# Operand start, one-word transfers ahead of weight reads, and regrouped sums in a linear-attention and two-FFN kernel

## The chip, the cores and the metric

The kernel runs on one core of a Trainium2 chip. The metric is the device time of one execution in microseconds. The engines are TensorE (PE in the rows; PEld is its weight load), VectorE (DVE), ScalarE (ACT), GpSimd (POOL) and SyncE (SP), which issues most transfers; POOL issues some on a queue of its own.

## The reference

All is fp32. Attention gives 4608 rows of 512 columns, and two feed-forward layers with squared ReLU follow, 512 to 2048 to 512 columns each:

```python
q_s = softmax(q, axis=-1); k_s = softmax(k, axis=seq)      # 8 x 8 heads, 576 x 64
kv  = einsum('bhsd,bhse->bhde', k_s, v)
x   = einsum('bhsd,bhde->bhse', q_s, kv)                    # -> 4608 x 512
x   = (max(x @ w_in1, 0) ** 2) @ w_out1
y   = (max(x @ w_in2, 0) ** 2) @ w_out2
```

## The kernel before

**Tiling.** The 4608 rows are worked in 9 blocks of 512 (numbered 0 to 8). The four weight matrices are called 0 to 3 in the order of use. Each is cut into 8 parts, and `W2_5` is part 5 of matrix 2, the second layer's first. A tile of the trace carries such a name: `W` a weight operand, `G` a hidden operand (`G0_8_7` is layer 0, block 8, part 7), `x` the second layer's input operand (`x0_0` and `x0_1` are the two halves of block 0), `v` the first layer's.

**Stages.** An opening stage does the attention and the first layer's first product in plain form for blocks 0 to 5; blocks 6 to 8 go through a *first crossing* (PSUM tiles `n`). Then come the *first sweep* (tiles `y`, matrix 1, about 474 to 816 us), the *second crossing* (tiles `m`, matrix 2, 816 to 1165 us, into which the last sums of the first sweep reach), and the *second sweep* (`y`, matrix 3, to the end). The blocks of the crossing and of the sweep after it follow each other without a gap, so that at 816 us the sums of block 8 of the first sweep and the first products of block 0 of the second crossing are worked together.

**Products.** Each 2 x 2 block product is formed from seven products in place of eight (`LEFT`, `RIGHT`, and the order of the products). Three PSUM banks hold a unit of a crossing: product 1; products 2, 4 and 7; products 5, 3 and 6 (`BANK`). A bank is used by the next product once its sum has been copied out. The name `m2_0_2` says: bank of product 2, block 0, unit 2; a unit is two weight parts, so unit 2 uses `W2_4` and `W2_5`. Each fp32 operand is split into a high and a low part and each product has three matmuls for each piece, so that a product of a crossing is 12 matmuls of 256 columns (`first_mm`, `passes`); all of these matmuls are issued in line 448.

**Operands.** An operand has seven combinations, 14 x 256 words with high and low. `combine` makes one out of a loaded tile: three additions of DVE into a scratch tile (`comb_add`, lines 97 to 106: 512, 512 and 256 columns), two copies of ACT that round to the high part (`comb_hi`, line 119: 512 and 1280 columns), two subtractions of DVE for the low part (`comb_lo`, line 125: 512 and 1280). `comb_hi` also chooses at which word of its buffer an x, v or G operand starts (`PLAIN` is 8, `EARLY` 4, `LATE` 40). The v operands start at `PLAIN`, and their row 0 of the high part, that of RIGHT index 0, starts four words earlier by a view `low`.

**Weights.** Some weight operands (`KEPT`, among them W2_0, W2_1, W2_2, W2_3, W2_5 and W2_7) were made earlier and stored ready in DRAM. `get_operand` (line 190) reads one, 1.8 MB, by a DMA of POOL's queue (`W<-o` in the rows) into one of eight slots. Two of these reads, and two for matrix 3, must not pass the load of a G tile in time; `touch` (line 186) stands ahead of each, an addition of one element by POOL that waits for the G tile. The other parts (W2_4, W2_6) are loaded as raw tiles by SP (`qx<-w`, line 177) and combined.

**Sums.** A unit's products become sums by ACT's copies of a bank (`copy`, line 476), POOL's or DVE's addition of two copies (`both`, line 479), DVE's `rest` (line 482), `summed` (line 488) and `plus` (line 518), POOL's `plus2` (line 521), then ReLU and square on ACT and a store.

**Order.** The kernel doesn't leave the order to a scheduler of the compiler: `schedule` is a list planner that is written in the kernel. Every operation is an `Op` with an engine, a cost in ns, a due time (`T` holds the stages' starts), the operations that it follows (`after`), the buffers that it uses (`Place`), for transfers their size (`lands`), `port` (whether it is counted as sharing DVE's and POOL's port) and `held` (a time before which it isn't taken). Each engine in the plan takes the ready operation of least due time, and the code is written out in that order for all engines, each of which then works strictly in order.

Of the kernel before, what the change touches and what calls it, by code (L numbers as in the profile page):

```python
# [48 lines left out]
def linear_attention_two_relu2_ffn(ctx: ExitStack, tc: tile.TileContext, q0, k0, eye, qh, kh, vh, wio, out):  # L49
# [58 lines left out]
    def comb_hi(key, q, x, tag):  # L108
        if key not in hls:
            if key[0] in "Gxv":  # L110
                t = pool.tile([P, 14 * HB + SHIFT], F32R, name=key, tag=tag)
                o = LATE + 4 * (key in ("G1_0_0", "G1_0_1", "G1_2_0")) if key[:2] == "G1" else EARLY if key == "G0_0_0" or key[:2] == "x0" else PLAIN
                hls[key] = t[:, o:o + 14 * HB].rearrange("p (a b n) -> p a b n", a=2, b=7)
                if key[0] == "v":
                    low[key] = t[:, o - 4:o - 4 + 2 * (HB + 4)].rearrange("p (a n) -> p a n", a=2)[:, :, :HB]
            else:
                hls[key] = pool.tile([P, 2, 7, HB], F32R, name=key, tag=tag)
        r, src = (slice(0, 2), q[:, 0:4:3]) if x == 0 else (slice(2, 7), cfs[key])
        nc.scalar.activation(out=low[key] if x == 0 and key in low else hls[key][:, 0, r], in_=src, func=AF.Copy)  # L119
# [63 lines left out]
    def put_operand(f, a):  # L183
        nc.sync.dma_start(out=ready_w[f, a], in_=f32(hls.pop(f"S{f}_{a}")))

    def touch(f, a, key):
        one = pool.tile([P, 1], F32, name=f"touch{f}_{a}", tag="kvm")
        nc.gpsimd.tensor_tensor(out=one, in0=gq[key][:, 0, 0:1], in1=gq[key][:, 0, 0:1], op=ALU.add)  # L188

    def get_operand(f, a, tag):  # L190
        hls[f"W{f}_{a}"] = pool.tile([P, 2, 7, HB], F32R, name=f"W{f}_{a}", tag=tag)
# [265 lines left out]
    def first_mm(l, j, u, i, place):  # L457

        k, o = (l, j, u), BANK[i]
        if i == o:  # L460
            m[k, o] = bank(place, f"{'nm'[l]}{i}_{j}_{u}")
        for s in range(2):
            w = hls[f"W{2 * l}_{2 * u + s}"]
            terms = []
            for kk in range(2):
                x, c = hls[f"{'vx'[l]}{j}_{kk}"], slice(kk * P, (kk + 1) * P)
                high = x[:, 0, RIGHT[i]] if l or RIGHT[i] else low[f"v{j}_{kk}"][:, 0]
                terms.append((w[:, 0, LEFT[i], c], w[:, 1, LEFT[i], c], high, x[:, 1, RIGHT[i]]))
            passes(m[k, o][:, s], terms, start=i == o and s == 0)

# [116 lines left out]
    def act(n, ps=False):  # L587
        return n * 0.823 + (174 if ps else 209)

    def dve(n):  # L590
        return n * 1.07 + 140
# [127 lines left out]

    combined = {}  # L720

    def combine(key, tag, due, engines, q, place, after, cfplace, new):

        hl = Place(tag)
        n = (512, 512, 256)
        adds = [op(e, gps(n[x]) if e == "POOL" else dve(n[x]), due - 5200 + 10 * x, lambda x=x, e=e: comb_add(key, q(), x, e, new), after, [place, cfplace], port=True)
                for x, e in enumerate(engines)]
        h0 = op("ACT", act(512), due - 4500, lambda: comb_hi(key, q(), 0, tag), after, [hl, place])
        h1 = op("ACT", act(1280), due - 3000, lambda: comb_hi(key, q(), 1, tag), adds, [hl, cfplace])
        l0 = op("DVE", dve(512), due - 2500, lambda: comb_lo(key, q(), 0), [h0], [hl, place], port=True)  # L730
        l1 = op("DVE", dve(1280), due - 1500, lambda: comb_lo(key, q(), 1), [h1], [hl, cfplace], port=True)
        combined[key] = [l0, l1], hl
# [73 lines left out]
    def weights(f, a, due):  # L806

        if (f, a) in KEPT:
            place = Place(slot_of(a))
            b = behind.get((f, a))  # L810
            if b:
                assert b in g_loads, (f, a)
            seen = op("POOL", 200, due - 9000, lambda: touch(f, a, b), [g_loads[b]], [g_place[b]]) if b else None
            l = op("POOL", 1400, due - 9000, lambda: get_operand(f, a, slot_of(a)), [*kept[f, a], seen, begun.get((f, a))], [place], lands=1792, port=False)
            combined[f"W{f}_{a}"] = [l], place
            return
        beside = Place(slot_of(a + 1)) if f == 0 and a not in (2, 7) else None
        place, new = quad_place("quad", 0, beside) if beside else quad_place(("qx", "qa")[a % 2] if f else "qc")
        after = [dma(due - 12000, lambda: get_w(f, a, new), 512, stashed[f, a], [place])]
        if beside:  # L820
            cf = Place("five", parent=beside), lambda: beside.area(4 * HB, 5 * HB).rearrange("p (a n) -> p a n", n=HB)
        else:
            cf = cf_place(("cf", ("att1", "att2")[a % 2], "att1", "att1")[f])
        combine(f"W{f}_{a}", slot_of(a), due, ("DVE",) * 3, lambda: wfs[f, a], place, after, *cf)

    kept, begun = {}, {}

# [172 lines left out]
    def first(l, j, u):  # L1000
        k, d = (l, j, u), when(2, j, u) if l else when(0, j, 4 * u)
        M, bk, tt = {}, {}, {}
        chain = chains[l]
        wx = [combined[f"W{2 * l}_{2 * u + s}"] for s in range(2)] + [combined[f"{'vx'[l]}{j}_{kk}"] for kk in range(2)]
        ready = [o for os, _ in wx for o in os]
        hl = [h for _, h in wx]
        bk = {i: Place("ps") for i in (2, 5, 1)}
        g = 1360

        def mm(i, due, after=()):  # L1010
            b = bk[BANK[i]]
            M[i] = op("PE", g, due, lambda: first_mm(l, j, u, i, b), [*ready, *after], [*hl, b])
            return M[i]

        def copy_of(i, due):
            tt[f"s{i}"] = t_place[k, f"s{i}"] = Place("t")
            return op("ACT", act(512, 1), due, lambda: copy(k, i), [M[i]], [tt[f"s{i}"], bk[i]])

        def out_of(q, o, due):
            if q in (0, 3):  # L1020
                o = op("ACT", act(512), due, lambda: relu(k, q), [o], [tt[q]])
            if l:
                o = op("ACT", act(512), due + 700, lambda: square(k, q), [o], [tt[q]])
            stored.setdefault((l, j, 2 * u), []).append(dma(due + 1500, lambda: put_g(k, q), 256, [o], [tt[q]]))
            stored[l, j, 2 * u + 1] = stored[l, j, 2 * u]


        mm(2, d, [chain[-3]] if chain else [])
        c2 = copy_of(2, d + g)
        mm(5, d + g, [M[2]])  # L1030
        c5 = copy_of(5, d + 2 * g)
        if (l, j) == (0, FIRST):
            s = op("DVE", dve(512), d + 3 * g, lambda: both(k, "DVE"), [c2, c5], [tt["s5"], tt["s2"]], port=True)
        else:
            s = op("POOL", gps(512), d + 3 * g, lambda: both(k), [c2, c5], [tt["s5"], tt["s2"]])
        mm(1, d + 4 * g, [M[5], *chain[-1:]])
        if (l, j, u) == (1, 0, 1):
            begun[2, 7] = M[1]
        e = op("DVE", dve(512), d + 5 * g, lambda: rest(k), [s, M[1]], [tt["s5"], bk[1]])
        for x, (i, q, c, y, f) in enumerate(((4, 2, c2, 7, 0), (3, 1, c5, 6, 3))):  # L1040
            o = BANK[i]
            mm(i, d + (5 + x) * g, [c, M[1 if x == 0 else 4]])
            tt[q] = t_place[k, q] = Place("t")
            r = op("ACT", act(512, 1), d + (6 + x) * g, lambda q=q, o=o: plain(k, q, o), [M[i]], [tt[q], bk[o]])
            out_of(q, r, d + (6 + x) * g + 3000)
            dy = d + (UNIT if l else SHORT / 4) + (2 + x) * g
            mm(y, dy, [r])
            tt[f] = t_place[k, f] = Place("t")
            r = op("DVE", dve(512), dy + g, lambda f=f, o=o: summed(k, f, o), [M[y], e], [tt[f], bk[o], tt["s5"]])
            out_of(f, r, dy + g + 3000)  # L1050
        chain[:] = [M[3], M[7], M[6]]
# [4 lines left out]
    def second(l, j, a):  # L1056
# [35 lines left out]
        for q, i, o, po in ((0, 7, 2, p21), (3, 6, 1, p12)):  # L1092
            tt[q] = t_place[k, q] = Place("t")
            if quick:
                y = op("DVE", dve(512), e + 2900, lambda q=q, o=o: plus3(k, q, o), [r, po], [tt[q], tt[o], tt["e"]], port=True)
                y = op("DVE", dve(512), e + 3000, lambda q=q, i=i: plus4(k, q, i), [y, M[i]], [tt[q], bk[i]])
            else:
                y = op("DVE", dve(512), e + 3000, lambda q=q, i=i: summed(k, q, i), [r, M[i]], [tt[q], bk[i], tt["s5"]])
                y = op("POOL", gps(512), e + 3600, lambda q=q, o=o: plus2(k, q, o), [y, po], [tt[q], tt[o]])
            y_stored[k, q] = dma(e + 5000, lambda q=q: put_y(k, q), 256, [y], [tt[q]])  # L1100

    spare = {}
# [139 lines left out]
```

## Time and profile before

| | us |
|---|---|
| median of 3 runs | 1509.36 (1506.9 to 1509.76) |
| profiled execution, its own time | 1511.11 |
| its span | 1509.3 |
| PE busy | 1487.6 |
| DVE busy | 1190.4 |
| ACT busy | 971.0 |
| POOL busy | 253.6 |

The span is the time between the first and the last instruction of the profiled execution, whose own time is longer by what lies around the span. PE was granted 0.999 of its full clock over the span. The share of busy time says which engine sets the pace over all; a single stop of PE is found in the list of its waits and in its timeline.

### The profile page before, as it was taken

What the parts mean: (1) busy time and instruction counts of PE and PEld (TensorE: products, weight loads), DVE (VectorE), ACT (ScalarE), POOL (GpSimd) and SP (SyncE); (2) the same over time, 40 slices, a digit from 0 to 9 for tenths busy, and PEclk for the clock granted to TensorE, in tenths of its full rate; (3) what the DMA queues carried; (4) which work ended last, traced back from release to release, by engine and by line L of the source; (5) the groups of instructions that cost most, each with busy time, mean ns of one, the idle gap of its engine ahead of it and who ended that gap; (6) DMA issues with size and microseconds to landing.
All of it is one profiled execution on the core that took longest, in us unless ns stands there. A gap on an engine that the chain in (4) does not pass through costs nothing.

```text
span 1509.3 us, 30549 instructions
## 1 busy us (share of the span) xinstructions
PE 1487.6 (99%) x12036; PEld 1414.4 (94%) x12036; DVE 1190.4 (79%) x1823; ACT 971.0 (64%) x1617; POOL 253.6 (17%) x193
## 2 busy tenths in 40 slices
PE   6999999999999999999999999999999999999998
PEld 5788888789999999999999999999999999999998
DVE  7998777899867999999986455444456999999996
ACT  8987767787765666666654788787777443444442
POOL 1001000000110111111113153243311111111110
PEclk9999999999999999999999999999999999999999
DMA  9888989986759444444447677677669644444441
GB/s 368 287 292 319 342 319 336 346 295 204 228 189 328 167 146 138 140 139 140 140 139 273 222 233 257 206 259 249 197 202 325 207 146 136 138 137 138 138 137 55
DMA packets 154144, 326.63 MB, mean 216 GB/s; under 512 B 13072, under 2 KB 84880, under 8 KB 151184
## 3 DMA queue, kind: packets, MB, share of 16 engines
q1 hardware_dynamic: 152128, 300.83, 59.5%
q0 software_dynamic: 1872, 23.86, 4.4%
q8 instruction: 94, 1.54, 0.4%
q14 instruction: 50, 0.41, 0.1%
HBM read 189.63 MB, written 135.00 MB: 215 GB/s over the span
## 4 chain that ended last, share of the span: by engine, by line
PE 90%; DMA 3%; ACT 3%; DVE 2%; issue 1%; POOL 1%; SPq 0%; DVEq 0%; ACTq 0%; POOLq 0%
PE y L448 44%; PE m L448 22%; PE h L448 15%; PE n L448 5%; PE xps L405 2%; PE kvps L334 1%; DMA qx<-w 1%; DMA W<-o 1%; POOL touch L188 0%; ACT w L153 0%; ACT wf L162 0%; DMA w<-w 0%; DMA w<-wio 0%; DMA qc<-w 0%; DMA att<-vh 0%
## 5 line engine op out<-in xcount | busy, mean ns | idle before, releaser
L448 PE MATMUL y<-G,W 128*128 128x256 f32 x3024 | 345.3, 277 | 2.0 <-DVE t L488 2.0
L448 PE MATMUL m<-x,W 128*128 128x256 f32 x3024 | 345.7, 277 | 1.5 <-DMA W<-o 1.5
L448 PEld LDWEIGHTS y<-G,W 128*128 128x128 f32 x3024 | 344.8, 188 | 2.2 <-DVE t L488 2.2
L448 PEld LDWEIGHTS m<-x,W 128*128 128x128 f32 x3024 | 345.1, 188 | 1.7 <-DMA W<-o 1.7
L448 PE MATMUL y<-W,G 128*128 128x256 f32 x3024 | 343.9, 276 | 0.0
L448 PEld LDWEIGHTS y<-W,G 128*128 128x128 f32 x3024 | 343.7, 188 | 0.0
L448 PE MATMUL h<-hl,w 128*128 128x512 f32 x1080 | 259.9, 396 | 3.4 <-DVE w L84 3.4
L448 PEld LDWEIGHTS h<-hl,w 128*128 128x128 f32 x1080 | 200.4, 188 | 49.6 <-DVE w L84 5.7
L479 POOL TENSOR_TENSOR ts<-ts,ts 128x512 f32<-128x512 f32 x61 | 93.5, 1533 | 750.2 <-DVE t L518 460.4
L119 ACT ACTIVATE G<-hl 128x1280 fp32r<-128x1280 f32 (+1 forms) x95 | 86.4, 926 | 115.9 <-PE y L448 65.5
L488 DVE TENSOR_TENSOR t<-m,ts 128x512 f32<-128x512 f32 x72 | 49.1, 688 | 97.5 <-PE m L448 77.9
L125 DVE TENSOR_TENSOR G<-hl,G 128x512 fp32r<-128x512 f32 (+1 forms) x95 | 108.7, 1149 | 16.2 <-ACT G L119 15.2
L448 PE MATMUL n<-v,W 128*128 128x256 f32 x1008 | 120.3, 280 | 0.0
L448 PEld LDWEIGHTS n<-v,W 128*128 128x128 f32 x1008 | 117.1, 188 | 2.1 <-issue 1.7
L491 ACT ACTIVATE t<-t 128x512 f32<-128x512 f32 x96 | 59.8, 628 | 56.2 <-DVE t L488 51.8
L494 ACT ACTIVATE t<-t 128x512 f32<-128x512 f32 x144 | 88.5, 627 | 2.3
L125 DVE TENSOR_TENSOR G<-cf,G 128x1280 fp32r<-128x1280 f32 x51 | 79.7, 1562 | 7.9 <-ACT G L119 7.3
L125 DVE TENSOR_TENSOR G<-att,G 128x1280 fp32r<-128x1280 f32 x49 | 75.9, 1549 | 8.4 <-ACT G L119 7.6
L319 POOL PARTITION_ALL_REDUCE m<-m x28 | 27.0, 964 | 310.5 <-DVE m L315 187.0
L435 ACT ACTIVATE r<-h 128x512 f32<-128x512 f32 x96 | 56.8, 593 | 20.6 <-PE h L448 14.8
L521 POOL TENSOR_TENSOR t<-t,t 128x512 f32<-128x512 f32 x34 | 61.0, 1817 | 42.0 <-DVE t L488 42.0
L119 ACT ACTIVATE G<-cf 128x1280 fp32r<-128x1280 f32 x51 | 64.5, 1265 | 5.6 <-DVE cf L106 5.5
(199 smaller groups left out, 1888.5 us busy)
## 6 DMA issues: line engine op xcount, KB each, us to landing
g<-t SPq DMA_DIRECT2D x192, 256.0 KB, 4.0
hl<-g SPq DMA_DIRECT2D x51, 512.0 KB, 3.8
raw<-wio SPq DMA_DIRECT2D x48, 512.0 KB, 5.3
g<-r SPq DMA_DIRECT2D x96, 256.0 KB, 5.2
W<-o POOLq DMA_DIRECT2D x13, 1792.0 KB, 9.5
y<-t SPq DMA_DIRECT2D x72, 256.0 KB, 2.4
w<-wf SPq DMA_DIRECT2D x64, 256.0 KB, 5.4
o<-S SPq DMA_DIRECT2D x9, 1792.0 KB, 8.3
```

Of the source, the lines that this page charges most:

```text
L119: nc.scalar.activation(out=low[key] if x == 0 and key in low else hls[key][:, 0, r], in_=src, func=AF.Copy)
L125: nc.vector.tensor_tensor(out=hl[:, 1, r], in0=src, in1=f32(hi), op=ALU.subtract)
L319: nc.gpsimd.partition_all_reduce(m[:, 1, :P], m[:, 0, :P], P, bass.bass_isa.ReduceOp.max)
L334: nc.tensor.matmul(ps[j * D:(j + 1) * D, 0:D + 1], k[lo:, c, j * D:(j + 1) * D], v[lo:, c, j, :], start=(c == 0), stop=(c == KC - 1),)
L405: nc.tensor.matmul(ps[:, r], begin[b % 2][p], q[:, r], start=True, stop=True)
L435: nc.scalar.activation(out=r0[j, f].rearrange("p a b -> p (a b)"), in_=m.pop(("h", j, f)), func=AF.Relu)
L448: nc.tensor.matmul(ps, a, b, start=start, stop=True, skip_group_check=True)
L479: (nc.gpsimd if eng == "POOL" else nc.vector).tensor_tensor(out=t[k, "s5"], in0=t[k, "s5"], in1=t[k, "s2"], op=ALU.add)
L488: nc.vector.tensor_tensor(out=temp(k, q), in0=m[k, i], in1=t[k, "s5"], op=ALU.add)
L491: nc.scalar.activation(out=t[k, q], in_=t[k, q], func=AF.Relu)
L494: nc.scalar.activation(out=t[k, q], in_=t[k, q], func=AF.Square)
L521: nc.gpsimd.tensor_tensor(out=t[k, q], in0=t[k, q], in1=t[k, o], op=ALU.add)
```

## The change

Seven edits, five of which change the program that is written out.

1. The x0 operands start at `PLAIN` instead of `EARLY`; row 0 of their high part, and of it alone, stays four words earlier, by the `low` view that the v operands have.
2. `touch` becomes a one-word DMA of POOL's queue that writes one element of the G tile to a small DRAM tile `seen`; the read that follows waits behind it in that queue and in the plan.
3. In the plan the read of W2_5 follows that of W2_3.
4. The additions and the first high part of W1_4 and W1_6 are held in the plan until 5 us before the first sweep's due start.
5. `both` of block 0, unit 0 of the second crossing goes from POOL to DVE.
6. The two `plus2` of the first sweep's block 8 are due 6 us later.
7. Loads of raw weight tiles are recorded, and an assertion is dropped; neither changes an instruction.

The diff, cut to its core:

```diff
-                o = LATE + 4 * (key in ("G1_0_0", "G1_0_1", "G1_2_0")) if key[:2] == "G1" else EARLY if key == "G0_0_0" or key[:2] == "x0" else PLAIN
+                o = LATE + 4 * (key in ("G1_0_0", "G1_0_1", "G1_2_0")) if key[:2] == "G1" else EARLY if key == "G0_0_0" else PLAIN
                 hls[key] = t[:, o:o + 14 * HB].rearrange("p (a b n) -> p a b n", a=2, b=7)
-                if key[0] == "v":
+                if key[0] == "v" or key[:2] == "x0":
                     low[key] = t[:, o - 4:o - 4 + 2 * (HB + 4)].rearrange("p (a n) -> p a n", a=2)[:, :, :HB]
...
+    seen = dram.tile([len(KEPT), 1], F32, name="seen", tag="seen")
+
     def touch(f, a, key):
-        one = pool.tile([P, 1], F32, name=f"touch{f}_{a}", tag="kvm")
-        nc.gpsimd.tensor_tensor(out=one, in0=gq[key][:, 0, 0:1], in1=gq[key][:, 0, 0:1], op=ALU.add)
+        t = gq[key] if len(key) == 3 else wfs[key]
+        x = KEPT.index((f, a))
+        nc.gpsimd.dma_start(out=seen[x:x + 1], in_=t[0:1, 0, 0:1])
...
-                high = x[:, 0, RIGHT[i]] if l or RIGHT[i] else low[f"v{j}_{kk}"][:, 0]
+                high = x[:, 0, RIGHT[i]] if RIGHT[i] or (l and j) else low[f"{'vx'[l]}{j}_{kk}"][:, 0]
...
+        for o in (*adds, h0):
+            o.held = held
...
-            seen = op("POOL", 200, due - 9000, lambda: touch(f, a, b), [g_loads[b]], [g_place[b]]) if b else None
-            l = op("POOL", 1400, due - 9000, lambda: get_operand(f, a, slot_of(a)), [*kept[f, a], seen, begun.get((f, a))], [place], lands=1792, port=False)
+            gate = op("POOL", 600, due - 9000, lambda: touch(f, a, b), [g_loads[b]], [g_place[b]], lands=1, port=False) if b else None
+            l = op("POOL", 1400, due - 9000, lambda: get_operand(f, a, slot_of(a)), [*kept[f, a], gate, *(combined["W2_3"][0] if (f, a) == (2, 5) else ()), begun.get((f, a))], [place], lands=1792, port=False)
...
+        combine(f"W{f}_{a}", slot_of(a), due, ("DVE",) * 3, lambda: wfs[f, a], place, after, *cf, held=T[1] - 5000 if (f, a) in ((1, 4), (1, 6)) else 0.0)
...
-        if (l, j) == (0, FIRST):
+        if (l, j) == (0, FIRST) or k == (1, 0, 0):
...
-                y = op("POOL", gps(512), e + 3600, lambda q=q, o=o: plus2(k, q, o), [y, po], [tt[q], tt[o]])
+                y = op("POOL", gps(512), e + 3600 + 6000 * (k == (0, NB - 1)), lambda q=q, o=o: plus2(k, q, o), [y, po], [tt[q], tt[o]])
```

The plan's order changes around 800 to 840 us, and a little near 1195 us; around 470 us no engine's order changes. Three places follow, word for word; `_9446` and the like are buffer numbers, `ts` and `t` are temporary tiles of sums, `att` and `cf` scratch tiles of `combine`, and `qx_7` is the raw tile of W2_6.

ACT at the turn from the first sweep to the second crossing (about 806 to 822 us), before:

```order
L119 ACTIVATE W2_4_9556<-att1_22_9570 128x1280
L119 ACTIVATE G0_8_7_9591<-att2_41_9601 128x1280
L476 ACTIVATE ts2_1_0_0_9660<-m2_0_0_9646 128x512
L476 ACTIVATE ts2_0_8_9674<-y2_0_8_9241 128x512
L476 ACTIVATE ts5_0_8_9682<-y5_0_8_9251 128x512
L476 ACTIVATE ts5_1_0_0_9742<-m5_0_0_9715 128x512
L485 ACTIVATE t2_1_0_0_9775<-m2_0_0_9646 128x512
```

After:

```order
L119 ACTIVATE W2_4_9557<-att1_22_9571 128x1280
L119 ACTIVATE G0_8_7_9591<-att2_41_9600 128x1280
L119 ACTIVATE W2_6_9657<-qx_7_9602 128x512
L479 ACTIVATE ts2_1_0_0_9667<-m2_0_0_9644 128x512
L479 ACTIVATE ts2_0_8_9676<-y2_0_8_9242 128x512
L479 ACTIVATE ts5_0_8_9686<-y5_0_8_9252 128x512
L119 ACTIVATE W2_6_9657<-att1_23_9659 128x1280
L479 ACTIVATE ts5_1_0_0_9747<-m5_0_0_9717 128x512
```

The two high parts of W2_6 move ahead of copies of the first units: the 512-column one ahead of all of them, the 1280-column one ahead of `ts5_1_0_0`. On DVE the three additions of W2_6 and its two low halves move likewise, ahead of `t2_0_8` and `t1_0_8`.

POOL's row from the last reads of the first sweep to the read of W2_7, before:

```order
L188 TENSOR_TENSOR touch2_2_9579<-qe_16_9448 128x1
L188 TENSOR_TENSOR touch2_3_9582<-qe_16_9448 128x1
L192 DMA W2_2_9593<-o2_2_118 128x3584
L192 DMA W2_3_9611<-o2_3_120 128x3584
L192 DMA W2_5_9629<-o2_5_121 128x3584
L479 TENSOR_TENSOR ts5_0_8_9682<-ts5_0_8_9682,ts2_0_8_9674 128x512
L479 TENSOR_TENSOR ts5_1_0_0_9742<-ts5_1_0_0_9742,ts2_1_0_0_9660 128x512
L521 TENSOR_TENSOR t0_0_8_9744<-t0_0_8_9744,t2_0_8_9696 128x512
L521 TENSOR_TENSOR t3_0_8_9747<-t3_0_8_9747,t1_0_8_9704 128x512
L479 TENSOR_TENSOR ts5_1_0_1_9856<-ts5_1_0_1_9856,ts2_1_0_1_9812 128x512
L192 DMA W2_7_9880<-o2_7_122 128x3584
```

After:

```order
L191 DMA seen_127<-qe_16_9449 1x1 x2
L195 DMA W2_2_9611<-o2_2_118 128x3584
L195 DMA W2_3_9629<-o2_3_120 128x3584
L482 TENSOR_TENSOR ts5_0_8_9686<-ts5_0_8_9686,ts2_0_8_9676 128x512
L524 TENSOR_TENSOR t0_0_8_9764<-t0_0_8_9764,t2_0_8_9701 128x512
L195 DMA W2_5_9800<-o2_5_121 128x3584
L524 TENSOR_TENSOR t3_0_8_9780<-t3_0_8_9780,t1_0_8_9730 128x512
L482 TENSOR_TENSOR ts5_1_0_1_9833<-ts5_1_0_1_9833,ts2_1_0_1_9818 128x512
L195 DMA W2_7_9886<-o2_7_122 128x3584
```

The additions `touch` are one-word transfers (`seen`), `both` of unit 0 (`ts5_1_0_0`) is gone to DVE, and the read of W2_5 stands behind the sum `t0_0_8` where it stood right behind that of W2_3.

PE's products of unit 2 of block 0 (each pair of rows of one weight part is half a product), before:

```order
L448 MATMUL m5_0_2_9921<-x0_0_9225,W2_5_9629 128x256 x3
L448 MATMUL m5_0_2_9921<-x0_1_9371,W2_5_9629 128x256 x3
L448 MATMUL m2_0_3_10035<-x0_0_9225,W2_6_9840 128x256 x3
L448 MATMUL m2_0_3_10035<-x0_1_9371,W2_6_9840 128x256 x3
L448 MATMUL m2_0_3_10035<-x0_0_9225,W2_7_9880 128x256 x3
L448 MATMUL m2_0_3_10035<-x0_1_9371,W2_7_9880 128x256 x3
L448 MATMUL m5_0_3_10052<-x0_0_9225,W2_6_9840 128x256 x3
L448 MATMUL m5_0_3_10052<-x0_1_9371,W2_6_9840 128x256 x3
L448 MATMUL m5_0_3_10052<-x0_0_9225,W2_7_9880 128x256 x3
L448 MATMUL m5_0_3_10052<-x0_1_9371,W2_7_9880 128x256 x3
L448 MATMUL m2_0_2_9904<-x0_0_9225,W2_4_9556 128x256 x3
L448 MATMUL m2_0_2_9904<-x0_1_9371,W2_4_9556 128x256 x3
```

After:

```order
L451 MATMUL m5_0_2_9923<-x0_0_9226,W2_5_9800 128x256 x3
L451 MATMUL m5_0_2_9923<-x0_1_9372,W2_5_9800 128x256 x3
L451 MATMUL m2_0_2_9906<-x0_0_9226,W2_4_9557 128x256 x3
L451 MATMUL m2_0_2_9906<-x0_1_9372,W2_4_9557 128x256 x3
L451 MATMUL m2_0_2_9906<-x0_0_9226,W2_5_9800 128x256 x3
L451 MATMUL m2_0_2_9906<-x0_1_9372,W2_5_9800 128x256 x3
L451 MATMUL m2_0_3_10046<-x0_0_9226,W2_6_9657 128x256 x3
L451 MATMUL m2_0_3_10046<-x0_1_9372,W2_6_9657 128x256 x3
L451 MATMUL m2_0_3_10046<-x0_0_9226,W2_7_9886 128x256 x3
L451 MATMUL m2_0_3_10046<-x0_1_9372,W2_7_9886 128x256 x3
L451 MATMUL m5_0_3_10064<-x0_0_9226,W2_6_9657 128x256 x3
L451 MATMUL m5_0_3_10064<-x0_1_9372,W2_6_9657 128x256 x3
```

In both, the first two rows end product 3 of unit 2, which writes the bank of product 5 again. The rows `m2_0_2` behind them are its product 7, which writes the bank of product 2 for the third time; they stand ahead of the first two products of unit 3 after, and behind them before.

## Rows read from the trace of the kernel before

**Rows 1.** The page: busy us of each engine; shares of the last chain.

```profile
PE 1487.6 (99%) x12036; PEld 1414.4 (94%) x12036; DVE 1190.4 (79%) x1823; ACT 971.0 (64%) x1617; POOL 253.6 (17%) x193
...
PE 90%; DMA 3%; ACT 3%; DVE 2%; issue 1%; POOL 1%; SPq 0%; DVEq 0%; ACTq 0%; POOLq 0%
```

**Rows 2.** PE's waits: releaser, then us in total, times, longest us.

```profile
PE y L448 <- DVE t L488: 2.0, 1, 2.0
PE m L448 <- DMA W<-o: 1.5, 1, 1.5
```

**Rows 3.** PE's timeline: start us, us, operation, count [idle before <-releaser].

```profile
474.42 10.84 PE L448 MATMUL y<-G,W 128*128 128x256 f32 x79 [2.05 <-DVE t L488]
...
816.22 6.60 PE L448 MATMUL m<-x,W 128*128 128x256 f32 x54
824.27 45.99 PE L448 MATMUL m<-x,W 128*128 128x256 f32 x389 [1.45 <-DMA W<-o]
```

**Rows 4.** The chain from 795 to 835 us: start us, us, what.

```profile
804.11 7.31 POOL touch L188
...
812.27 11.96 DMA W<-o
```

**Rows 5.** Windows: us, PE, PEld, DVE, ACT, POOL busy (count), PE clock, DMA share, GB/s.

```profile
470.00:476.00 6.00, 3.95 (x29) 3.75 (x28) 4.64 (x7) 2.88 (x4) 0.53 (x1) 0.89 0.82 272
476.00:480.00 4.00, 4.00 (x29) 4.00 (x29) 3.53 (x4) 3.95 (x6) 0.00 (x0) 0.75 0.99 292
...
822.00:826.00 4.00, 2.55 (x21) 2.34 (x21) 1.70 (x2) 1.91 (x5) 0.81 (x1) 1.00 1.06 420
```

**Rows 6.** Windows, line 448 alone: us, PE and PEld busy (count), clock, DMA, GB/s.

```profile
500.00:800.00 300.00, 300.00 (x2649) 300.00 (x2649) 1.00 0.47 150
826.00:856.00 30.00, 30.00 (x254) 30.00 (x253) 1.00 0.79 275
870.00:900.00 30.00, 30.00 (x267) 30.00 (x266) 1.00 0.69 215
```

**Rows 7.** Window in the first crossing, tile n alone: PE, PEld, DVE, ACT, clock.

```profile
420.00:450.00 30.00, 30.00 (x264) 30.00 (x263) 6.22 (x9) 8.12 (x14) 1.00 0.60 199
```

**Rows 8.** POOL's timeline: a read's issue, and `both` of the first sweep's block 8.

```profile
786.68 0.53 POOL L192 DMA_DIRECT2D W<-o  x1 [1.48 <-PE y L448]
...
816.00 1.28 POOL L479 TENSOR_TENSOR ts<-ts,ts 128x512 f32<-128x512 f32 x1 [2.66 <-DVE t L518]
```

**Rows 9.** DVE's timeline: beside that issue, and first and last beside `touch`.

```profile
786.70 1.48 DVE L125 TENSOR_TENSOR G<-att,G 128x1280 fp32r<-128x1280 f32 x1
...
804.19 0.68 DVE L102 TENSOR_TENSOR att<-qx 128x512 f32<-128x512 f32 x1
...
809.87 1.48 DVE L125 TENSOR_TENSOR G<-att,G 128x1280 fp32r<-128x1280 f32 x1
```

**Rows 10.** Transfers issued at 808.6, 785.6, 1137.0, 1136.3, 811.7, 827 us; last, us to landing.

```profile
qx<-w SPq DMA_DIRECT2D x1, 512.0 KB, 3.7
...
qd<-g SPq DMA_DIRECT2D x1, 512.0 KB, 11.4
...
qx<-w SPq DMA_DIRECT2D x1, 512.0 KB, 9.2
...
W<-o POOLq DMA_DIRECT2D x1, 1792.0 KB, 9.2
...
W<-o POOLq DMA_DIRECT2D x1, 1792.0 KB, 7.6
...
xq<-y SPq DMA_DIRECT2D x1, 512.0 KB, 12.7
```

**Rows 11.** SP's timeline: the load of qx_7 (W2_6).

```profile
808.62 0.32 SPq L177 DMA_DIRECT2D qx<-w  x1
```

**Rows 12.** ACT's timeline: copies at the turn, and a 1280-column high part of x.

```profile
812.40 1.28 ACT L476 ACTIVATE ts<-y 128x512 f32<-128x512 f32 x2
...
837.77 1.28 ACT L119 ACTIVATE x<-cf 128x1280 fp32r<-128x1280 f32 x1
```

More of the change, by code (lines that the diff above doesn't have):

```diff
@@ L720, in linear_attention_two_relu2_ffn, with combine @@
     combined = {}
-    def combine(key, tag, due, engines, q, place, after, cfplace, new):
+    def combine(key, tag, due, engines, q, place, after, cfplace, new, held=0.0):
         hl = Place(tag)
@@ L810, in weights @@
             b = behind.get((f, a))
-            if b:
-                assert b in g_loads, (f, a)
-            seen = op("POOL", 200, due - 9000, lambda: touch(f, a, b), [g_loads[b]], [g_place[b]]) if b else None
-            l = op("POOL", 1400, due - 9000, lambda: get_operand(f, a, slot_of(a)), [*kept[f, a], seen, begun.get((f, a))], [place], lands=1792, port=False)
+            gate = op("POOL", 600, due - 9000, lambda: touch(f, a, b), [g_loads[b]], [g_place[b]], lands=1, port=False) if b else None
+            l = op("POOL", 1400, due - 9000, lambda: get_operand(f, a, slot_of(a)), [*kept[f, a], gate, *(combined["W2_3"][0] if (f, a) == (2, 5) else ()), begun.get((f, a))], [place], lands=1792, port=False)
             combined[f"W{f}_{a}"] = [l], place
@@ L819, in weights @@
         after = [dma(due - 12000, lambda: get_w(f, a, new), 512, stashed[f, a], [place])]
+        g_loads[f, a], g_place[f, a] = after[0], place
         if beside:
@@ L823, in weights @@
             cf = cf_place(("cf", ("att1", "att2")[a % 2], "att1", "att1")[f])
-        combine(f"W{f}_{a}", slot_of(a), due, ("DVE",) * 3, lambda: wfs[f, a], place, after, *cf)
+        combine(f"W{f}_{a}", slot_of(a), due, ("DVE",) * 3, lambda: wfs[f, a], place, after, *cf, held=T[1] - 5000 if (f, a) in ((1, 4), (1, 6)) else 0.0)
     kept, begun = {}, {}
```

## Prediction

> **What bounds the kernel now.** I read the page first. TensorE (PE) is busy 99% of the span and holds 90% of the chain that ended last [rows 1], so an edit pays only where it ends a stop of PE or shortens its matmuls, and costs only where it makes a new stop. The list of PE's waits came next [rows 2]: two of them lie where the change works, 2.0 us for a sum of line 488 and 1.5 us for a weight read (W<-o). PE's timeline places them [rows 3]: the first ends at 474.42, the second at 824.27, after 54 matmuls begun at 816.22. The windows give the clock around both [rows 5]: 0.89 and 0.75 of full in the ten microseconds about the first stop, 1.00 after the second. The chain through the second stop [rows 4] tells its cause: POOL's two one-element additions (`touch`) begin at 804.11, when ACT's square is done, and the first takes 7.31 us; then the reads are issued, and the second of them (W2_3) takes 11.96 us.
>
> The change was laid over the trace with the order of each engine, before and after. Durations below come from the profiled execution (1511.11 us, span 1509.3); the median of the runs shown, 1509.36, lies 1.75 us lower, and I subtract that at the end.
>
> **The held sums (W1_4, W1_6).** The orders of all five engines are the same around 470 us: the hold forbids nothing that was done. The 2.05 us stop at 474 and its slow clock stay. Zero.
>
> **The x0 operands' start.** Block 0 of the second crossing multiplies x0 from 816 to about 856; its matmuls stand 30.00/254 = 118 ns apart from 826 to 856, and 30.00/267 = 112.4 ns from 870 to 900, when x1 is used, 300.00/2649 = 113.3 ns over the first sweep [rows 6]. The trace doesn't say why. The first crossing's products, whose v operands already start at the place that x0 is moved to and have the same early view of row 0, stand 30.00/264 = 113.6 ns apart [rows 7]. That is the nearest row, so I expect x0's matmuls to come to it. Of the 336 matmuls on x0 (4 units of 7 products of 12), 32 use row 0's early view and stay; 304 x 5.7 ns = 1.75 us gained. Bounds: 0, if it is the transfers of that stretch (share 0.79 against 0.69 [rows 6]), and 1.75.
>
> **One-word transfers for `touch`.** The additions held POOL from 804.11 to 811.42 [rows 4], while DVE ran sums with two inputs from 804.19 to 811.35 without a gap (the first and last of these are rows 9). A POOL-queue DMA issued at 786.68, beside DVE's subtraction at 786.70, took 0.53 us [rows 8, 9]. Two such transfers put the reads' issue at 804.11 + 2 x 0.55 = 805.2 and 805.75, 6.5 us earlier. The second read landed 11.96 us after its issue at 812.27, and the first 7.6 us after its own at 811.71 [rows 4, 10]; from 805.75 with the former W2_3 is there at 817.7, five microseconds before PE wants it at 816.22 + 6.60 = 822.8 [rows 3]. The 1.45 us stop goes. Gained 1.45; bounds 0 and 1.45. The two other touches (1137 and 1170 us) gate reads for which PE doesn't wait; zero.
>
> **What is late next: qx_7.** This is where the order changes most. Before, SP's load qx<-w at 808.62 (qx_7, the weights of W2_6) ran alone, ahead of the reads, and took 3.7 us [rows 10, 11]; what uses it stood behind all y sums. After, DVE finishes the low half that frees its buffer two microseconds sooner (it is moved ahead of three additions and a low half, 3 x 0.5 + 0.6 by rows 9), so the load goes out at about 806.4, just *behind* two reads of 1.8 MB. And ACT's `W2_6<-qx_7` now stands ahead of the three copies `ts2_1_0_0`, `ts2_0_8`, `ts5_0_8`, as DVE's four sums of W2_6 stand ahead of `t2_0_8`. Loads of this size with a read ahead took 9.2 us (one read, issued 0.72 us earlier, itself 9.2) and 11.4 us (a read ahead and a second close behind) [rows 10]. So qx_7 lands at L between 815.6 and 817.8; alone it would be 810.1. I take 816.7, inside the former pair, since two reads are ahead here.
>
> The Trainium skill ("DMA: Bandwidth & Descriptors", section "Queues, rings and completion order") says that each DMA engine goes round robin between the rings it has work for, a packet at a time. Read as even shares of time, qx_7 would need twice its 3.7 us and land near 814; the 9.2 and 11.4 us of this trace disagree with even shares, since the read's packets are larger. That case is rival A.
>
> **First stop (m5_0_0).** The second-crossing products begin at 816.22 with `m5_0_0`, whose bank is freed by `ts2_0_8`. ACT's two copies ended at 813.68 before [rows 12]; after, ACT waits for L, then 0.6 (hi) and two copies of 0.6: L + 1.7 = 818.4. Stop 2.2 us; bounds 0 (L under 814.5) and 3.4. The 2.05 us stop at 474 was followed by a slower clock: 6 x 0.11 + 4 x 0.25 = 1.7 us lost [rows 5]; the 1.45 us stop was not. 2.2 is nearer to the former, so +1.7; bounds 0 and 1.7.
>
> **Second (W2_5).** POOL issues W2_5 now after its sum `t0_0_8`, which waits for DVE's row: three additions, two low halves, `t2`, `t1`, `both`, two `rest`, `t0`, at 0.6 us for 512 columns and 1.4 for 1280 [rows 9], 8.7 us after L in all with ACT's share, then 1.4 us on POOL (1.28 for its like [rows 8]). Issue L + 10.1, landing 7.6 to 9.2 later [rows 10]. PE wants it 11.5 products (of 12 x 113.5 ns = 1.362 us) after m5_0_0: L + 1.7 + 15.7 = L + 17.4, and 1.7 later if the clock fell. So 0.3 to 1.9 without a slow clock, 0 with it; I take 0 beside the +1.7.
>
> **Third (unit 2's product 7).** It is moved two products forward and needs ACT's copy `t2_1_0_2`; ACT's row has the hi of x1 ahead of it, whose loads (xq) go out near 827 among W2_5 and W2_7. One such took 12.7 us [rows 10]: 839.7, then two operands of 0.6 + 1.3 us each [rows 12] and the copy, about 844.2. PE arrives at L + 27.9 = 844.6 with the slow clock, 842.9 without. Bounds 0 and 5 (if W2_7, sent after W2_5, takes its 9.2 us first); I take 1.2.
>
> `both` on DVE (0.6 [rows 9] in place of POOL's 1.28 [rows 8]) and the later plus2 are inside these counts. The regrouping near 1195 us moves sums and products where PE's list of waits has nothing that long [rows 2]; one 512-column sum that comes late costs up to 0.6 [rows 9], so bounds 0 and 0.6, taken zero.
>
> **Sum.** -1.45 - 1.75 + 2.2 + 1.7 + 0 + 1.2 = +1.9: 1513.0 in the profiled execution's scale, 1511.3 in the median's.
>
> **Rivals.**
> A, faster: the load shares well and L is under 812.5, so neither first nor second stop comes: -3.2, or -2.0 with the third: 1506.2 to 1507.4. For it: SP's queue holds nothing else at 806. Against it: both loads with reads ahead [rows 10].
> B, slower: W2_5 and W2_7 back to back hold the xq loads past 841. The third stop is then 5 us, and the clock falls again (1.7): 1511.3 + 3.8 + 1.7 = 1516.8. It decides from a landing of xq at 841 on; for it speak the 12.7 us of an xq load behind reads [rows 10], against it that PE had no wait on x1 before [rows 2].
> C, the one-word transfer doesn't free POOL: POOL's issue is held through DVE's sums as the addition was, until 811.42 [rows 4]. Then qx_7 is ahead of the reads as before, the 1.45 us stop stays, and -1.75 and +1.2 remain: 1508.8. Against it the 0.53 us at 786.68 [rows 8].
> The Trainium skill ("SBUF — State Buffer", section "🔬 SBUF: two separate sides") warns of this: descriptors of POOL's queue are written by GpSimd, which waits for the port it shares with VectorE. It adds that a VectorE operation with two SBUF inputs bars only GpSimd work that reads SBUF, which agrees with the 7.31 us of the addition and the 0.53 us of the issue.
> D, the pitch doesn't come from the start: 1.75 back, 1513.0, inside my own case.
>
> **Chances.** My forecast 0.5 (1508.5 to 1513.5), A 0.2, B 0.2, C 0.1. The range from 1506.0 to 1517.0 takes in A's end and B. A measurement here tells 0.2%, 3.0 us, from no change: faster is below 1506.3, which only A at its best reaches, with the spread of the runs: 0.17. Slower is above 1512.4: B, and my case with the pitch unchanged or the third stop larger, 0.36. Same 0.47.
>
> **What would show it.** W2_2 issued near 805, W2_3 landed before 820, no wait of PE on W<-o at 824. qx_7 landed at 815 to 818 and ACT waiting for it ahead of `ts2_1_0_0`; a stop of PE at 816 of about 2 us with a clock under 1.00 behind it. Pitch 113 ns from 826 to 856. The stop at 474 unchanged. I am wrong if qx_7 lands by 813, or if PE waits anywhere that the orders show alike.

## The result and the profile after

The changed kernel is slower. Its median is 1517.07 us (1512.75 to 1528.44, 10 runs) against 1508.94 us (10 runs beside it), a ratio of 1.0058 with a 95% interval of 1.0031 to 1.0085. A second timing gave 1515.89 against 1507.43, 1.0051 (1.0028 to 1.0075). Slower had 0.36 in the forecast, "same" 0.47; the first median lies just past the upper end of the range, 1517.0, the second within it. Some executions lie 8 us or more above the fastest of their sample, which widens the intervals: three of ten and two of twelve of the changed kernel, two of ten, four of 35, none of 28 and five of 23 of before. The profiled execution of after took 1514.48 us, its span is 1512.7.

PE's list of waits after (releaser: us in total, times, longest; compare [rows 2]):

```profile
PE m L451 <- ACT t L488: 3.8, 1, 3.8
PE m L451 <- ACT ts L479: 3.4, 1, 3.4
```

The wait for W<-o is gone, as forecast, and so is the 2.0 us for a sum of line 488 (now 491), which was not. In their place stand two waits for ACT. PE's timeline places them (compare [rows 3]):

```profile
815.60 26.66 PE L451 MATMUL m<-x,W 128*128 128x256 f32 x216 [3.37 <-ACT ts L479]
846.03 34.22 PE L451 MATMUL m<-x,W 128*128 128x256 f32 x285 [3.77 <-ACT t L488]
```

Each is followed by a slow clock, which the windows show (columns as in [rows 5]: the third number from the end is the granted clock):

```profile
812.00:816.00 4.00, 0.63 (x5) 0.44 (x4) 2.04 (x4) 2.05 (x5) 0.00 (x0) 0.94 0.30 120
816.00:820.00 4.00, 4.00 (x24) 4.00 (x24) 3.50 (x5) 1.80 (x3) 0.54 (x1) 0.63 0.19 66
...
844.00:848.00 4.00, 1.97 (x10) 1.98 (x11) 4.00 (x7) 3.63 (x8) 0.00 (x0) 0.78 0.28 95
848.00:852.00 4.00, 4.00 (x30) 4.00 (x30) 2.53 (x3) 2.46 (x4) 0.00 (x0) 0.79 0.32 107
```

Against a full clock that is 4 x (0.06 + 0.37) = 1.7 us lost behind the first stop and 4 x (0.22 + 0.21) = 1.7 behind the second.

**The first stop.** ACT's timeline after shows what it waits for (start, us, operation, [idle before <-releaser]):

```profile
813.95 0.63 ACT L119 ACTIVATE W<-qx 128x512 fp32r<-128x512 f32 x1 [8.84 <-DMA qx<-w]
814.49 0.58 ACT L479 ACTIVATE ts<-m 128x512 f32<-128x512 f32 x1
814.96 1.08 ACT L479 ACTIVATE ts<-y 128x512 f32<-128x512 f32 x2
```

ACT stands 8.84 us for qx_7, and the copies that free PE's next bank come behind it. The load itself (the last number: us from issue to landing; compare the first line of [rows 10]):

```profile
qx<-w SPq DMA_DIRECT2D x1, 512.0 KB, 11.6
```

**The second stop.** The loads of x1, the next block's operand, take 13.1 us at the median (12.8 and 13.5), and ACT waits for both ahead of the copy (845.40) that PE waits for:

```profile
xq<-y SPq DMA_DIRECT2D x2, 512.0 KB, 13.1
```

```profile
840.87 0.63 ACT L119 ACTIVATE x<-xq 128x512 fp32r<-128x512 f32 x1 [1.52 <-DMA xq<-y]
842.15 0.63 ACT L119 ACTIVATE x<-xq 128x512 fp32r<-128x512 f32 x1 [0.64 <-DMA xq<-y]
...
845.40 0.57 ACT L488 ACTIVATE t<-m 128x512 f32<-128x512 f32 x1
```

SP's timeline dates their issue:

```profile
802.28 0.32 SPq L177 DMA_DIRECT2D qx<-w  x1
816.82 2.90 SPq L541 DMA_DIRECT2D y<-t  x2
822.86 0.53 SPq L501 DMA_DIRECT2D g<-t  x1
824.45 0.36 SPq L541 DMA_DIRECT2D y<-t  x1
824.91 1.20 SPq L501 DMA_DIRECT2D g<-t  x1
826.30 1.72 SPq L541 DMA_DIRECT2D y<-t  x1
828.07 1.09 SPq L548 DMA_DIRECT2D xq<-y  x2
```

In the kernel before they go out at 825.29, in a trace that is 4.2 us behind this one at the turn:

```profile
825.29 2.52 SPq L545 DMA_DIRECT2D xq<-y  x2
```

The xq loads stand in SP's queue behind the last two y stores, and these wait for POOL's `t0_0_8` and `t3_0_8`, which wait for qx_7's sums. So the late qx_7 makes x1 late as well. The reads of W2_5 and W2_7 go out on POOL's queue just ahead of them:

```profile
824.37 0.57 POOL L195 DMA_DIRECT2D W<-o  x1
827.70 0.57 POOL L195 DMA_DIRECT2D W<-o  x1
```

**The base.** The kernel before, profiled a second time, has no stop at 474 us:

```profile
471.85 18.34 PE L448 MATMUL y<-G,W 128*128 128x256 f32 x160
```

Its span is 1505.1 and its time 1506.88; everything else, the 1.5 us for W2_3 included, is as in the first profile. So the stop at 474 and its slow clock, nearly 4 us in the first profile, are not in every execution of the kernel. Against this profile the account of after closes: 3.4 + 1.7 + 3.8 + 1.7 for the two stops, less 1.5 for W2_3 and 1.5 for the pitch of x0's matmuls, is +7.6, and 1512.7 - 1505.1 = 7.6. Edits 4 to 6 and the regrouping near 1195 us were not run by themselves; beside the two stops the account leaves nothing for them.

### The profile page after: what moved, and what is told of

It is laid out like the page before. It is cut to its first block, busy times and chain, and to the rows that moved or that the text cites. A ratio compares the mean times of both kernels' runs of the same rounds, so it can differ in the third digit from the quotient of the medians.

```text
span 1512.7 us, 30551 instructions
## 1 busy us (share of the span) xinstructions
PE 1487.5 (98%) x12036; PEld 1414.2 (93%) x12036; DVE 1189.8 (79%) x1824; ACT 969.9 (64%) x1617; POOL 247.0 (16%) x192
## 4 chain that ended last, share of the span: by engine, by line
PE 73%; DVE 10%; DMA 9%; ACT 5%; issue 2%; SPq 0%; POOL 0%; DVEq 0%; ACTq 0%; POOLq 0%
PE y L451 44%; PE m L451 22%; PE n L451 6%; DMA w<-wf 4%; DMA qc<-w 2%; DMA xq<-y 1%; PE h L451 1%; DVE wf L167 1%; DMA qx<-w 1%; DVE W L125 1%; DVE S L125 1%; ACT wf L162 1%; DVE qT L401 1%; DVE qs L388 0%; ACT qso L365 0%
## 5 line engine op out<-in xcount | busy, mean ns | idle before, releaser
L125 DVE TENSOR_TENSOR G<-hl,G 128x512 fp32r<-128x512 f32 (+1 forms) x95 | 109.9, 1161 | 16.9 <-ACT G L119 15.6
L438 ACT ACTIVATE r<-h 128x512 f32<-128x512 f32 x96 | 56.6, 592 | 15.2 <-PE h L451 11.4
```

Of the source, the lines that this page charges most:

```text
L125: nc.vector.tensor_tensor(out=hl[:, 1, r], in0=src, in1=f32(hi), op=ALU.subtract)
L438: nc.scalar.activation(out=r0[j, f].rearrange("p a b -> p (a b)"), in_=m.pop(("h", j, f)), func=AF.Relu)
```

## The experiments

**again.** The changed kernel once more.

> The changed kernel itself, profiled and timed a second time. Theory: its loss sits at the turn from the first sweep to the second crossing, in two stops of PE (about 3.4 us at 815 for ACT behind the load of qx_7, about 3.8 us at 846 for ACT behind the loads of x1), each with 1.5 to 2 us of slow clock; both come back here within 1 us. The stop at 474 us, 2.05 us in the profile of before and absent in that of after, is in no engine's order and so is chance: it may or may not be there. Rival: the loss is spread over places that the one profile of after doesn't show; then a stop of PE stands here that neither profile has, and the two at the turn are of another size.

```profile
815.54 26.96 PE L451 MATMUL m<-x,W 128*128 128x256 f32 x216 [2.90 <-ACT ts L479]
845.85 24.35 PE L451 MATMUL m<-x,W 128*128 128x256 f32 x198 [3.35 <-ACT t L488]
```

PE's timeline has both stops again, half a microsecond shorter each, and none at 474. The rival got something too: between 1163 and 1250 us this execution lost 3.2 us against that of after, only 0.3 of it in a stop (at 1169; more on the rest in the last section).

**before_again.** The kernel before once more.

> The kernel before, profiled a second time. Theory (the stop at 474 us is chance, from when one load lands): it is absent or of another size, and the span is that of the first profile less what is missing there, down to 1505.6; the stop for W2_3 at 824 us is there within 0.3 us of 1.5. Rival: the stop is part of the kernel before, 2 us again.

As shown above: no stop at 474, the stop for W2_3 of 1.5 us in its place, span 1505.1. The stop at 474 is chance. It grows with one load of qx, on the same order: 2.05 us with a load of 13.1 us from issue to landing in the first profile, 1.42 with 12.4 in x0_start below, 0.6 to 0.7 with 11.6 or 11.7 in x0_word_dma, held_w26 and w25_early, none with 10.5 in after and 9.4 here.

**x0_start.** The operand's start alone.

```diff
-  ... else EARLY if key == "G0_0_0" or key[:2] == "x0" else PLAIN
+  ... else EARLY if key == "G0_0_0" else PLAIN
...
```

> The kernel before with the x0 operands' start alone changed (the order of all engines is as before). Theory: x0's matmuls come to 113.4 ns apart from 826 to 856 us (265 in 30 us, before 254), 1.75 us less, ratio 0.9988. Rival: the transfers of that stretch set the pitch, the count stays at 254 and the time at 1.0000.

The ratio is 1.0002 (0.998 to 1.0024), which can't tell 1.75 us from nothing (and the profiled execution has the stop at 474 again, 1.42 us). The trace tells more. From 826 to 850 us (x0's block ends at 852 here) PE does 210 matmuls on x0:

```profile
826.00:850.00 24.00, 24.00 (x210) 24.00 (x210) 1.00 0.83 291
```

The kernel before has 203 there, at the same share of transfers:

```profile
826.00:850.00 24.00, 24.00 (x203) 24.00 (x202) 1.00 0.83 292
```

The 265 in 30 us that were expected would be 212 in 24. In x0_start PE does 87 in the first 10 us and 125 in the other 14; why the first stretch gains less is not shown.

**word_dma.** The kernel before with the one-word transfers alone; plan and order untouched.

```diff
-        nc.gpsimd.tensor_tensor(out=one, in0=gq[key][:, 0, 0:1], in1=gq[key][:, 0, 0:1], op=ALU.add)
+        nc.gpsimd.dma_start(out=seen[x:x + 1], in_=gq[key][0:1, 0, 0:1])
...
```

> The kernel before with the one-element additions ahead of the reads made one-word transfers, the plan and the order untouched. Theory: the reads go out 6.5 us earlier, PE's 1.45 us stop for W2_3 goes; the load of qx_7, issued near 808.6, now stands behind three reads and lands near 820, where DVE first wants it at 820.5, so that 0 to 2 us are lost there: time between -1.45 and +0.5 us of before, ratio 0.999 to 1.0003. Rival: the transfers themselves are what makes the changed kernel slow; then this kernel is slower by 5 us or more, 1.003 or above.

The time is unclear, 1.0016 (0.9987 to 1.0045), and does not rule the rival out. The trace is clear: PE's timeline runs through the turn without a stop.

```profile
812.51 57.75 PE L450 MATMUL m<-x,W 128*128 128x256 f32 x491
```

qx_7 is as late as in the changed kernel, 10.6 us from issue to landing, with three reads ahead of it; here only the sums of W2_6 wait for it, which stand behind those that PE needs. So in the trace neither the transfers nor a late qx_7 alone make a stop; the next kernel, which has the same transfers, rules out a loss of 5 us by its time too.

**x0_word_dma.** Both of these edits on the kernel before.

> The kernel before with its plan untouched and two edits alone: the one-word transfers and the x0 operands' start. Theory: the two gains that single runs showed in the trace add up, no stop between 800 and 860 us and 265 matmuls in 30 us on x0: 3 us less than a run of before without a stop at 474, ratio 0.998. Rival: the gains overlap or faster x0 matmuls reach W2_5 or W2_6 before these land; then a new stop of about 1 us or more stands in that stretch.

1505.6 against 1508.04 us, ratio 0.9988 (0.9973 to 1.0003), and PE's timeline has no stop from 800 to 870. This kernel and word_dma settle the pitch, since they have the same transfers beside the same matmuls. x0 at its new start (line 450 alone, 30 us of x0's block):

```profile
817.00:847.00 30.00, 30.00 (x265) 30.00 (x264) 1.00 0.82 286
```

and at the old one:

```profile
814.00:844.00 30.00, 30.00 (x254) 30.00 (x254) 1.00 0.81 283
```

113.2 against 118.1 ns at the same share of transfers: it is the operand's start. Over 304 matmuls that is 1.5 us.

**held_w26.** The changed kernel with the sums of W2_6 held.

```diff
-  held=T[1] - 5000 if (f, a) in ((1, 4), (1, 6)) else 0.0)
+  held=T[1] - 5000 if (f, a) in ((1, 4), (1, 6)) else T[2] + 9000 if (f, a) == (2, 6) else 0.0)
```

> The changed kernel with the sums of W2_6 held in the plan behind the last sums of the first sweep, so that no copy on ACT and no sum on DVE waits for qx_7. Theory: the stop at 815 (3.4 us) and its slow clock (1.5 us) go, 4.9 us less than the changed kernel; the stop at 846 for x1's loads stays, since W2_5, W2_7 and those loads still go out together: ratio to before about 1.001 to 1.003. Rival: another stop takes the place of the first (W2_5 or W2_6 too late) and the time stays that of the changed kernel, 1.005.

1509.61 against 1507.43 us, 1.0021 (0.9992 to 1.0049). qx_7 lands 11.0 us after its issue, and nobody on PE's path waits for it: the first stop is gone, and the second stays, 2.1 us without a slow clock.

```profile
812.75 24.83 PE L451 MATMUL m<-x,W 128*128 128x256 f32 x216
839.72 30.53 PE L451 MATMUL m<-x,W 128*128 128x256 f32 x266 [2.14 <-ACT t L488]
```

The xq loads go out at 820.25 here, eight microseconds sooner than in after, since the y stores ahead of them are in time. Yet the first lands 14.3 us later, with W2_5 issued at 818.40 just ahead and W2_7 at 823.17 just behind:

```profile
xq<-y SPq DMA_DIRECT2D x1, 512.0 KB, 14.3
```

**added_back.** The changed kernel's order with POOL's additions in place of the transfers.

```diff
-        nc.gpsimd.dma_start(out=seen[x:x + 1], in_=t[0:1, 0, 0:1])
+        nc.gpsimd.tensor_tensor(out=one, in0=gq[key][:, 0, 0:1], in1=gq[key][:, 0, 0:1], op=ALU.add)
...
```

> The changed kernel with its order of all engines kept and only the one-word transfers ahead of the reads made POOL's one-element additions again. Theory (the load of qx_7 is late because it goes out behind two reads): the additions hold the reads until DVE's run ends, so that qx_7 goes out 4 to 5 us ahead of them and lands about 4 us after its issue; the stop of PE at 815 for ACT (2.9 to 3.4 us) and its slow clock go, and a stop for W2_3 of 1.5 to 3 us comes in their place, with or without a slow clock. The stop behind x1's loads stays at 2 to 4 us. Ratio to before 1.001 to 1.005. Rival (the order of ACT and DVE by itself makes the first stop, wherever the load lands): the stop for ACT stays at 2 us or more.

1512.8 against 1508.04 us, 1.0029 (1.0020 to 1.0039). The reads go out 8.6 us later (809.77) and qx_7 alone at 802.35; it takes 3.5 us:

```profile
qx<-w SPq DMA_DIRECT2D x1, 512.0 KB, 3.5
```

With the same order of ACT and DVE the first stop is gone; W2_3 makes another, 4.85 us and not the 1.5 to 3 that I expected, with a slow clock behind it (0.53 of full from 824 to 828):

```profile
812.14 6.44 PE L448 MATMUL m<-x,W 128*128 128x256 f32 x54
823.43 46.82 PE L448 MATMUL m<-x,W 128*128 128x256 f32 x391 [4.85 <-DMA W<-o]
```

So the order makes a stop only with the load behind the reads. The expectation that x1's stop stays was a miss: xq goes out at 820.5, lands at 832.5 and 833.7, and PE, held up already, doesn't wait for it. A stop of that length ahead hides the second one; without any, in held_w26, 2.1 us of it are left.

**w25_early.** The changed kernel with W2_5 read right behind W2_3.

```diff
-  *(combined["W2_3"][0] if (f, a) == (2, 5) else ())
+  gates[2, 3] if (f, a) == (2, 5) else None
...
```

> The changed kernel with the read of W2_5 right behind that of W2_3, as in the kernel before. Theory (x1's loads are late because W2_5 and W2_7 go out just ahead of them): only W2_7 is ahead of x1's loads, they land 3 us sooner or more, and the second stop (3.3 to 3.8 us at 846) with its slow clock of 1.7 us goes or falls under 1 us; the first stop stays at 3 us or grows, as qx_7 stands behind three reads. Ratio to before 1.001 to 1.003. Rival (product 7 of unit 2, moved ahead, makes the second stop by its place alone): the stop stays over 2 us.

1510.4 against 1508.04 us, 1.0014 (0.9997 to 1.0031). The first stop is there, and no second:

```profile
816.85 53.40 PE L451 MATMUL m<-x,W 128*128 128x256 f32 x454 [2.94 <-ACT ts L479]
```

xq goes out at 828.29, as late as in after, but with W2_7 alone ahead of it, and the first takes 9.2 us in place of 12.8:

```profile
xq<-y SPq DMA_DIRECT2D x1, 512.0 KB, 9.2
```

The rival is not ruled out by this, since product 7 of unit 2 stands no longer where the changed kernel has it: with the read's place the planner put it back behind the first two products of unit 3. In after it comes right behind the 216 matmuls between the two stops. Here PE has begun 217 by 843.02 without a wait (columns as in [rows 6]), and ACT's copy that product 7 needs begins only at 844.23:

```profile
816.85:843.02 26.17, 26.17 (x217) 26.17 (x217) 0.94 0.70 246
```

```profile
844.23 0.58 ACT L488 ACTIVATE t<-m 128x512 f32<-128x512 f32 x1
```

In the early place it would have waited some 1.7 us, by an estimate from the ends of that copy (844.8) and of the 216 matmuls (843.2). So this kernel took away the late landing and the early place together. The early place without a late landing makes no stop: added_back has it.

**held_w26_w25.** Both repairs in one kernel.

> Both of these repairs: the sums of W2_6 held behind the last sums of the first sweep, and the read of W2_5 right behind that of W2_3. Theory: no stop of PE over 0.5 us between 800 and 860 us, the read of W2_3 in time and x0's matmuls at 113.4 ns: 3 us less than a run of before without a stop at 474, ratio 0.998. Rival: a third load comes late (the reads only change which one), a stop of over 1 us stays and the ratio is 1.000 or above.

1504.99 us (1504.01 to 1505.45, 7 runs) against 1508.04, ratio 0.9974 (0.9964 to 0.9985): faster than before and than the changed kernel, and without a stop at the turn. Product 7 of unit 2 stands late here too.

**both_again and both_no_x0.** The same once more, and beside it with the x0 start undone.

> The kernel with the sums of W2_6 held and W2_5 read right behind W2_3, a second time, for the one with the x0 start undone to stand beside it. Theory: no stop over 0.5 us between 800 and 860 us and a ratio to before of 0.996 to 0.9985 again. Rival: the first timing was luck, ratio 0.999 or above.

> The kernel with the sums of W2_6 held and W2_5 read right behind W2_3, with the x0 operands' start undone (EARLY again). Theory: x0's matmuls fall back from 265 to 254 in 30 us, 1.4 to 1.5 us over the whole block, and nothing else changes: slower by 1.5 us than the same kernel with the new start, run beside it. Rival: the transfers set the pitch, and the two are the same.

1504.37 us again for the first, 0.9968 (0.9943 to 0.9993) of before; PE's timeline has no stop from 800 to 870:

```profile
812.12 58.13 PE L451 MATMUL m<-x,W 128*128 128x256 f32 x509
```

The other one's median is 1505.48, 1.1 us more, in the direction of the 1.5 us that the pitch gives; its own ratio, 0.9987 (0.9960 to 1.0013), doesn't tell it from before. Its trace, where x0's block begins at 827, has the 254 matmuls in 30 us that were expected:

```profile
829.00:859.00 30.00, 30.00 (x254) 30.00 (x253) 1.00 0.79 274
```

## Why the prediction was wrong

- **Which is late next: right in kind.** qx_7 behind the two reads, ACT and DVE standing for it, a stop of PE at `m5_0_0` with a slow clock behind it: all are in the trace. L was dated 1.3 us early (10.3 us from issue to landing taken, 11.6 measured; the row with a second read close by, 11.4, was the nearer one, and I took a middle). The stop was 3.4 where the sum has 2.2. The slow clock cost the 1.7 that was taken.
- **W2_5: right.** Issued at 824.37, 10.5 us after qx_7's landing at 813.87 (10.1 forecast), and no stop for it.
- **Gains: nearly right.** W2_3's 1.5 us as forecast, by reads that went out from 801.21 on, 1.1 us after POOL was let go; x0's pitch 1.5 where 1.75 was taken, and x0_word_dma and word_dma show that it is the start and not the transfers. The 1.75 was a slip: I named 113.6 ns as the nearest row and then multiplied by 5.7, the difference to the 112.4 of x1; 304 x 4.5 ns is 1.4.
- **The step that failed is the third stop.** The sum has 1.2 us; 3.8 came, and 1.7 of slow clock behind it that the sum doesn't have. These 4.3 us are most of the 5.7 by which the profiles (+7.6 against before_again) passed the sum's +1.9; the first stop is 1.2 more. The prediction dated the xq loads "near 827", which is where the second of them stands in the kernel before. They went out from 828.07 on in a trace that runs 4.2 us ahead there, thus near 832: I counted what the late qx_7 does to POOL's sums, but not to the y stores that follow these in SP's queue, ahead of xq. From there they took 12.8 and 13.5 us, little more than the 12.7 that was taken. The outcome is rival B's (a third stop and a second slow clock), which was given 0.2 and stood at 1516.8, but by another way: a later issue and not a longer hold. Even the 1.2 didn't follow from the times given: a copy at 844.2 against PE at 844.6, with the slow clock that the sum has, is no stop at all (1.3 without it).
- **What the third stop hangs on.** A late landing of xq and the early place of product 7 of unit 2, which the prediction had seen. With the early place there are 3.3 to 3.8 us in the changed kernel, 2.1 in held_w26, where xq goes out early between W2_5 and W2_7, and none in added_back, where xq landed by 833.7 and PE came to product 7 only at 844.2. With product 7 in its old place there is no stop, in w25_early or in held_w26_w25. Of the 3.8 us the place makes up to 2.7, by an estimate: in the old order PE would have had two more products to do first (24 x 113.3 ns). No kernel was run with the place alone taken back.
- **The base.** I took the first profile's 474 stop for part of the kernel and moved from its 1511.11 to the median by subtracting 1.75. That stop is chance; the profile without it stands at 1506.88, and the medians of the samples of 10 to 35 lie at 1507.4 to 1508.9. "The stop at 474 unchanged" was wrong for that reason, though the hold does nothing to the order, as said.
- **Rivals.** A fell with qx_7's 11.6 us, C with the reads' issue at 801.21, while DVE's two-input additions ran. On the two citations: the Trainium skill ("DMA: Bandwidth & Descriptors", section "Queues, rings and completion order") has each DMA engine go round robin between rings by whole packets. Read as even shares of time, that would have had qx_7 take about twice its 3.7 us; it took 11.6. What the Trainium skill ("SBUF — State Buffer", section "🔬 SBUF: two separate sides") says, that a VectorE operation with two SBUF inputs bars only GpSimd work that reads SBUF, agrees with this trace: beside such sums the two one-word transfers together took 1.06 us on POOL, and the first addition 7.31 in the kernel before.

## What to carry to other kernels

A gate that holds back large reads can be what lets a small load pass: before making it cheaper, look which loads go out in the time that it took, and who stands behind these on an engine that works in order. Follow a late transfer through every queue to the end of its row, stores on SP included, since what stands behind them is late too. When a planner writes the order, compare the whole order after each single edit: a repair meant for one read also moved the product that waited. And take a second profile of the kernel before, or compare the profiled time with a larger sample, before counting a stop as part of it.

## What the runs showed of the hardware

In the profiled execution of both_no_x0 (span 1518.7) the whole first sweep runs at another pitch, with no wait and a full clock:

```profile
500.00:800.00 300.00, 300.00 (x2549) 300.00 (x2548) 1.00 0.42 138
```

The same instructions of the sweep in both_again:

```profile
500.00:800.00 300.00, 300.00 (x2649) 300.00 (x2648) 1.00 0.45 150
```

That is 117.7 against 113.3 ns a matmul. It begins at about 474 us and ends with the sweep, which takes 13.2 us longer (474.00 to 827.31, against 471.98 to 812.12); that is most of the 16.9 us between the two spans. The loss from 1163 to 1250 us in again is of the same kind: from 1170 to 1240 PE does 596 matmuls there (117.4 ns). The step is nearly that of x0's start (118.1 against 113.2 ns), but the kernel of again is that of after, whose profile has 618 matmuls in the same stretch. What sets it off was not found.
